# A convolution kernel's set-up: h's first FFT stage reads h in place, and table indices are made in another order

## The chip, the cores and the metric

One Trainium2 chip, one core of it. The metric is the device time of one execution in microseconds (us); the time before is the median of three runs. Five engines work side by side, each through its own queue in order: TensorE (PE; its weight loads are listed as PEld), VectorE (DVE), ScalarE (ACT), GpSimd (POOL) and SyncE (SP). TensorE writes its results to PSUM, from where VectorE or ScalarE move ("evict") them to SBUF.

## The reference, cut to what matters

```
# first part: a long causal convolution along the sequence, by FFT
B, S, D = 8, 5696, 128 ;  L = 2 * S
y = irfft(rfft(x, n=L, axis=1) * rfft(h, n=L, axis=0)[None], n=L, axis=1)[:, :S, :]
# second part, with x = y
theta  = x @ w_theta
zr, zi = x * cos(theta), x * sin(theta)
y = einsum('ts,bsd->btd', w_tok_r, zr) + einsum('ts,bsd->btd', w_tok_i, zi)
u = x + y
out = u + maximum(u @ w_ch, 0)
```

x is 8 x 5696 x 128 and h is 5696 x 128 in float32; w_tok_r and w_tok_i are 5696 x 5696. The change lies in the first part, and there in what is done once: the spectrum of h and the tables.

## The kernel before

**The FFT.** The length of 11392 is split into N1 = 178 and N2 = 64. The 5696 samples lie as NB = 89 partitions of N2 = 64 samples each. Stage a (`stage_a`) is a DFT over the 89 partitions: for each channel one product whose stationary operand (the weights) is the 89 x 128 block of data, and whose moving operand is the table f1_t (89 x 180, cosines and sines of K1 = 90 frequencies). Four channels make a chunk in one PSUM buffer of two banks; there are 16 chunks (64 channels) and four such buffers. Each chunk is evicted, with a change of layout, by ScalarE or by VectorE: `on_dve` lists the chunks that VectorE takes. Stage 2 (`f2`) multiplies by the table w_t2, 32 small products a chunk in 12 chunks (`CHK`), two halves of the array at a time. Stage b (`stage_b`) multiplies x's spectrum by h's into u_t and v_t (line 400, one product for each). Stages c and d go back to time.

**How h is treated.** h is loaded by two DMAs into the first 8192 columns of u_t (lines 122 to 125), as [n, half, d] in float16: 64 samples n, two halves of the channels, 64 channels d. VectorE then copies it (line 291) into h16 with the halves outermost, so that for each d the 128 weights (half, n) stand at one constant step. `h_chunk` evicts h's stage 2: ScalarE writes the real part to the tiles hs (line 326), VectorE the other part to h16 under the name h_later (line 327), which is used a second time for that. `h_other` exchanges halves by 18 DMAs on SyncE's queue, and `h_store` puts the rest in memory.

**The tables.** w_t2 is made in three parts: `w_turns`, `w_angles` and `w_sines`, and then on VectorE alone `w_rest` (lines 203 to 211), four instructions a part. `e_index` (three GpSimd instructions: iota, product, sum) makes the arguments for one of seven steps of the table e_t, and `e_table` turns them into sines on VectorE and ScalarE; four steps' arguments fit at a time, so steps 4 to 6 wait for earlier ones to be used. `r_table` makes the two small tables r_u and r_v; its arguments are seven GpSimd instructions each.

**What sets the order.** From line 143 on, VectorE, ScalarE and GpSimd run in the order of the program (a manual schedule). At line 486 GpSimd leaves that order and is placed by the scheduler; VectorE and ScalarE stay in it through stage b of the first group of x. There are eight groups of x (four pairs of batches, two halves of the channels); group 0's stage a is the list a0, its stage b is b0, and `load_x(1)` loads the next group into the same single buffer x16, 16 DMAs on GpSimd's queue. `woven` interleaves lists of steps by position.

Before the change the order is: the copy into h16; w_rest 1; h's stage a (chunks 4, 6, 8, 10, 12 and 14 on VectorE); w_rest 2; h's stage 2; e_index 0 to 3 and the arguments of r_table (which the scheduler puts among them on GpSimd, from 23.6 to 43.2 us); x's stage a with e_table 0 after its tenth chunk; load_x(1); e_index 4; stage b with r_table.

Of the kernel before, what the change touches and what calls it, by code (L numbers as in the profile page):

```python
# [10 lines left out]
F32 = mybir.dt.float32  # L11
# [12 lines left out]
def kernel(  # L24
# [10 lines left out]
    nc = tc.nc  # L35
    B, S, D = x.shape
    assert D == 128
    P = 128
# [119 lines left out]
    def up(t, k, eng=nc.vector):  # L158
        eng.tensor_scalar(k, t, MAGIC, None, op0=add)
# [43 lines left out]
    def w_rest(b):  # L203
        s0 = WS * b
        here = w_t2[:, s0:s0 + WS]
        two = here[:, :, :2 * N2].rearrange("p k (f a n) -> p k f a n", f=2, a=2)
        nc.vector.tensor_scalar(two[:, :, :, 1], two[:, :, :, 0], odd, None, op0=mult)
        nc.vector.tensor_scalar(here[:, :, 2 * N2:], here[:, :, :N2], -1.0, None, op0=mult)
        for p0 in (0, 64):
            nc.vector.tensor_copy(w_t2[p0:p0 + 64, KH + s0:KH + s0 + WS],  # L210
                                  w_t2[64 - p0:P - p0, s0:s0 + WS])
# [29 lines left out]
    def stage_a(lhs, on_dve=()):  # L241

        st = {}

        def chunk(q):
            if q == 0:
                st["a"] = fa.tile([P, 2 * K1, HD], F16, tag="a", name="a_")
            ps = psum()
            for i in range(4):
                nc.tensor.matmul(ps[:, i // 2, (i % 2) * 2 * K1:(i % 2 + 1) * 2 * K1], lhs(q + i), f1_t[:NB],  # L250
                                 start=True, stop=True)
            a_out = st["a"][:, :, q:q + 4].rearrange("p k (a q) -> p k a q", a=2)
            a_in = ps[:, :, :4 * K1].rearrange("p a (q k) -> p k a q", q=2)
            if q // 4 in on_dve:
                nc.vector.tensor_copy(a_out, a_in)
            else:
                nc.scalar.activation(a_out, a_in, AF.Copy)
        return [lambda q=q: chunk(q) for q in range(0, HD, 4)], st
# [28 lines left out]
    w_in = [s1.tile([P, P], F32, name=f"w_in{q}") for q in range(2)]  # L287
    for w_, t in ((moe_w_theta, w_in[0]), (moe_w_ch, w_in[1])):
        nc.gpsimd.dma_start(t, w_[:, :])
    for d0 in range(0, HD, 32):  # L290
        nc.vector.tensor_copy(h16[:NB, :, :, d0:d0 + 32],
                              u_t[:NB, :N2 * D].rearrange("p (n h d) -> p h n d", h=2, d=HD)[:, :, :, d0:d0 + 32])
    steps, a_h = stage_a(lambda q: h16[:NB].rearrange("p h n d -> p (h n) d")[:, :, q], (4, 6, 8, 10, 12, 14))
    w_rest(1)
    for f in steps:
        f()
    w_rest(2)

    nc.gpsimd.memset(u_t[:, UVW:], 0.0)
    nc.gpsimd.memset(v_t[:, UVW:], 0.0)  # L300
# [40 lines left out]
    e_t = fc.tile([P, EN, 2, NB], F16)  # L341
    sgn = fc.tile([P, N2], F32)

    def r_table(n_, r_):
        t, k = (s1.tile([P, 2 * N2], F32, name=f"r_{n_}{q}") for q in "tk")
        index(k, [[0, 2], [1, N2]], 0)
        nc.gpsimd.tensor_scalar(t, k, lane[:, 0:1], 1.0 / N2, op0=mult, op1=mult)
        for q0 in range(2):
            for q1 in range(2):
                a_ = t[64 * q0:64 * q0 + 64, 64 * q1:64 * q1 + 64]  # L350
                nc.gpsimd.tensor_scalar(a_, a_, 0.25 * (1 + (1 - n_ if q0 else n_) + q0 - q1), None, op0=add)
        up(t, k, nc.gpsimd)
        below_one(t, k)
        sine(k, t, 1)
        nc.scalar.activation(r_[:, :N2 + EN], k[:, :N2 + EN], AF.Copy, scale=0.125)
        nc.scalar.activation(r_[:, N2 + EN:], k[:, N2 + EN:], AF.Copy, scale=-0.125)
# [116 lines left out]
                h_other(c0, n)  # L473
    for c0, n in BATCH:
        h_store(c0, n)
    for e_ in E_STEPS[:4]:
        e_index(*e_)
    for t, dst, mul in ((w_in[0], w_theta_sb, 1.0 / (2.0 * math.pi)), (w_in[1], w_ch_sb, 1.0)):
        nc.gpsimd.tensor_scalar(dst, t, mul, None, op0=mult)
    for n, f in enumerate(a0):  # L480
# [1 line left out]
        if n == 9:  # L482
            e_table(*E_STEPS[0])
    load_x(1)
    e_index(*E_STEPS[4])
    in_order.close()
    in_order.enter_context(tc.manual_schedule(engines={mybir.EngineType.DVE, mybir.EngineType.Activation}))
    woven(b0, ([s_table, lambda: r_table(0, r_u), lambda: r_table(1, r_v)], 0.0, 0.6),
# [797 lines left out]
```

## Time and profile before

| | |
|---|---|
| median of 3 runs | 2045.61 us (2044.21 to 2046.22) |
| the profiled execution | 2043.46 us, span 2041.7 us, mean granted clock 0.986 |
| TensorE, VectorE, ScalarE, GpSimd busy | 95%, 77%, 32%, 48% of the span |
| h's load lands | 10.2 and 10.4 us after the issues at 1.28 and 2.32 us |
| h's stage a on TensorE | 16.09 to 25.9 us |
| h's stage 2 on TensorE | 26.79 to 35.9 us |
| x's stage a, stage b, stage c begin | 36.26, 45.13, 66.47 us |

Times in the profile are counted from the start of the span. "Idle before, with a releaser" names what ended a wait; a wait for several things is put down to the one that came last. Products are pipelined: the duration shown of one contains the way through the array, and the distance between starts says how fast they go. A granted clock of 0.50 is half clock. No clock event is recorded ahead of 32 us; the column reads 1.00 there whatever the clock was. In tile names the profile cuts digits: f_t is f1_t, h is h16, w_t is w_t2.

### The profile page before, as it was taken

To read this page: it belongs to the slowest core of one execution; us is meant where nothing else is said; L and a number is where in the kernel's file an instruction comes from. 1 tells how busy PE (TensorE), PEld (TensorE's weight loads), DVE (VectorE), ACT (ScalarE), POOL (GpSimd) and SP (SyncE) were. 2 spreads that over 40 slices of the span, in tenths; PEclk is the share of its full clock that TensorE was granted. 3 is DMA by queue.
4 is the path that set the end of the run, shared out by engine and by line. 5 is a ranking of instruction groups with operands and counts; after the bars stand their busy time and mean duration, and the time that the engine had idled before them with its cause. 6 is when DMAs were issued, how large, how long until landed. Compare 5 with 4: busy or idle time off the path is not lost.

```text
span 2041.7 us, 41287 instructions
## 1 busy us (share of the span) xinstructions
PE 1938.2 (95%) x15664; PEld 1074.5 (53%) x15841; DVE 1573.3 (77%) x2890; ACT 654.2 (32%) x1004; POOL 973.8 (48%) x1744
## 2 busy tenths in 40 slices
PE   5799999799999999999999998999999999999998
PEld 5688888654444444444444443444444444444444
DVE  8777778777788888888876757867777786777767
ACT  6788888862232333233200000011111111111111
POOL 8523421485353545454666454453544545354450
PEclk9799999899999999999999999999999999999999
DMA  9969975999898989999999799796977969788793
GB/s 117 62 74 130 92 83 167 262 264 187 158 178 174 175 170 168 176 174 180 166 168 157 121 258 210 111 154 125 154 139 133 160 123 155 132 148 145 133 156 85
DMA packets 491239, 312.56 MB, mean 153 GB/s; under 512 B 182983, under 2 KB 456007, under 8 KB 490055
## 3 DMA queue, kind: packets, MB, share of 16 engines
q0 software_dynamic: 322608, 158.13, 61.2%
q1 hardware_dynamic: 162448, 140.25, 24.2%
q10 hardware_dynamic: 5984, 11.54, 1.6%
q8 instruction: 124, 2.03, 0.4%
q14 instruction: 75, 0.61, 0.1%
HBM read 354.89 MB, written 90.82 MB: 218 GB/s over the span
## 4 chain that ended last, share of the span: by engine, by line
PE 63%; DVE 4%; DMA 3%; issue 2%; POOL 2%; ACT 0%; DVEq 0%; SPq 0%
PE m L1223 59%; POOL ring L627 2%; DVE c L1230 1%; DMA ring<-in_moe_w_tok_i_dram 1%; PE v L925 1%; PE utp L918 1%; PE m L1227 1%; DVE wt L838 1%; DVE b L776 1%; DMA ring<-in_moe_w_tok_r_dram 1%; PE theta_ps L514 0%; PE tpz L866 0%; DMA wl<-in_moe_w_tok_i_dram 0%; PE m L1110 0%; PE m L1144 0%
## 5 line engine op out<-in xcount | busy, mean ns | idle before, releaser
L627 POOL DMA_DIRECT2D ring<-in_moe_w_tok_i_dram x720 | 387.6, 546 | 652.4 <-DVE wt L838 581.6
L627 POOL DMA_DIRECT2D ring<-in_moe_w_tok_r_dram x720 | 386.6, 548 | 137.2 <-DVE wt L838 82.8
L838 DVE STREAM_TRANSPOSE wt<-ring 128x384 f32<-128x384 f32 (+2 forms) x720 | 359.5, 524 | 116.1 <-PE m L1223 67.5
L1223 PE MATMUL m<-b,wt 128*128 128x512 bf16 x1599 | 385.0, 379 | 4.2 <-DVE wt L838 1.7
L1223 PEld LDWEIGHTS <-wt 128*128 128x128 bf16 x1804 | 175.9, 98 | 218.8 <-DVE wt L838 7.5
L1230 DVE TENSOR_TENSOR c<-c,m 128x512 f32<-128x512 f32 x412 | 265.9, 671 | 0.4 <-PE m L1223 0.4
L920 ACT ACTIVATE ring<-utp 128x512 bf16<-128x512 bf16 x85 | 50.7, 597 | 582.2 <-PE utp L918 582.2
L137 POOL DMA_DIRECT2D x<-in_x_dram x128 | 99.1, 788 | 142.3 <-PE ps L250 132.4
L420 PE MATMUL ps<-r_u,u_t 128*128 128x128 f16 x1024 | 125.6, 221 | 5.3 <-DVE u_t L400 2.4
L421 PE MATMUL ps<-r_v,v_t 128*128 128x128 f16 x1024 | 124.6, 221 | 0.2
L915 ACT ACTIVATE ub<-c 128x512 bf16<-128x512 f32 x88 | 55.1, 628 | 192.1 <-DVE c L1185 113.5
L1144 PE MATMUL m<-b,wt 128*128 128x512 bf16 x465 | 109.8, 381 | 7.2 <-DMA b<-zz 2.7
L421 PEld LDWEIGHTS <-v_t 128*128 128x128 f16 x1024 | 101.1, 99 | 5.2 <-issue 3.7
L420 PEld LDWEIGHTS <-u_t 128*128 128x128 f16 x1024 | 101.2, 99 | 3.3 <-DVE u_t L400 3.3
L398 ACT ACTIVATE xs<-ps 128x1024 f16<-128x1024 f32 x96 | 91.6, 982 | 9.6 <-PE ps L274 3.3
L400 DVE TENSOR_TENSOR u_t<-xs,hs 128x1024 f16<-128x1024 f16 x96 | 64.3, 670 | 31.4 <-ACT xs L398 29.1
L1144 PEld LDWEIGHTS <-wt 128*128 128x128 bf16 x528 | 50.6, 98 | 67.4 <-issue 6.5
L516 ACT ACTIVATE red<-theta_ps,magic 128x512 f32<-128x512 f32 (+1 forms) x46 | 31.6, 687 | 137.0 <-PE theta_ps L514 102.8
L268 PEld LDWEIGHTS <-w_t 64*128 64x128 f16 x3240 | 58.9, 101 | 22.2 <-issue 16.4
L868 ACT ACTIVATE ring<-tpz 128x512 bf16<-128x512 bf16 (+1 forms) x46 | 27.5, 597 | 130.6 <-PE tpz L866 115.6
L400 DVE TENSOR_TENSOR v_t<-xs,hs 128x1024 f16<-128x1024 f16 x96 | 63.8, 665 | 0.0
L776 DVE TENSOR_TENSOR b<-b 128x1024 bf16<-128x1024 bf16 x100 | 61.4, 682 | 0.0
(2934 smaller groups left out, 3796.5 us busy)
## 6 DMA issues: line engine op xcount, KB each, us to landing
ring<-in_moe_w_tok_r_dram POOLq DMA_DIRECT2D x352, 96.0 KB, 4.5
ring<-in_moe_w_tok_i_dram POOLq DMA_DIRECT2D x352, 96.0 KB, 4.7
ring<-in_moe_w_tok_r_dram POOLq DMA_DIRECT2D x352, 80.0 KB, 4.4
ring<-in_moe_w_tok_i_dram POOLq DMA_DIRECT2D x352, 80.0 KB, 3.8
cp_hbm<-c SPq DMA_DIRECT2D x88, 256.0 KB, 2.5
c<-cp_hbm SPq DMA_DIRECT2D x88, 256.0 KB, 4.5
out_dram<-c SPq DMA_DIRECT2D x88, 256.0 KB, 4.2
yy<-y_hbm SPq DMA_DIRECT2D x84, 128.0 KB, 2.4
```

The source lines that it names most:

```text
L137: nc.gpsimd.dma_start(x16[p0:p1, e, n0:n0 + 16, :HD], bass.AP(tensor=src.tensor, offset=src.offset + (p0 * N2 + n0) * D + dh * HD, ap=[[N2 ...
L268: nc.tensor.matmul(ps[:, e, j * HD:(j + 1) * HD], w_t2[rows, slot(e, c0 + j), N2 * (1 - ri):N2 * (3 - ri)], a_st["a"][rows, ri * K1 + c0 + ...
L398: nc.scalar.activation(xs[:, :, :, :ck], ps, AF.Copy)
L400: nc.vector.tensor_tensor(uv[r][:, :, :, c0:c0 + ck], xs[:, :, :, :ck], hv[:, r:r + 1].to_broadcast([P, 2, HD, ck]), op=mult)
L420: nc.tensor.matmul(o, u_t[:, at:at + P], r_u, start=True, stop=False)
L421: nc.tensor.matmul(o, v_t[:, at:at + P], r_v, start=False, stop=True)
L627: nc.gpsimd.dma_start(wb[32 * i:32 * i + 32, :ng, :nj * 64], bass.AP(tensor=a.tensor, offset=a.offset + row0 * S + p * H + i * QR + j0 * 6 ...
L776: return [lambda f=f, x=x: f(*x) for f, x in ((nc.vector.tensor_sub, (bt[M3], b12, b22)), (nc.vector.tensor_sub, (bt[M4], b21, b11)), (nc. ...
L838: nc.vector.transpose(wt.rearrange("p j t r -> p (j t r)").bitcast(F32).rearrange("p (j g t) -> p g j t", j=TJ, g=4)[:, :ng, :nj], wb[:, : ...
L1144: nc.tensor.matmul(ms[n // 2 * 2 + h], a[n][:, j, :, r], bts_of[p][jj][n % 2 * 2 + h][:, r, :], start=(n % 2 == 0 and jj == 0 and r == 0), ...
L1223: nc.tensor.matmul(ms[q], a[q][:, j, :, r], bts[jj][q][:, r, :], start=(jj == 0 and r == 0), stop=(jj == NJ - 1 and r == 1 and q not in left))
L1230: nc.vector.tensor_tensor(c, z, ms[q], op=op)
```

## The change

Three things are changed. h's copy into h16 is left out: stage a takes a list of weights per channel, for h two 89 x 64 blocks straight from u_t (64 samples at a step of 128 elements), and multiplies each with f1_t into its own half of the output partitions; for x nothing changes. VectorE now takes chunks 11, 13 and 15 of h's stage a and ScalarE the other 13, and w_rest 1 and 2 are written after the fourth and the eighth chunk; on VectorE's queue that is w_rest 0, 1, 2 and then the three chunks. And on GpSimd's queue the arguments come as e_index 0, both r_table's (split off as `r_index`), e_index 1, the two weights, load_x(1), then e_index 2, 3 and 4.

```diff
@@ stage_a, chunk
-                nc.tensor.matmul(ps[:, i // 2, (i % 2) * 2 * K1:(i % 2 + 1) * 2 * K1], lhs(q + i), f1_t[:NB],
-                                 start=True, stop=True)
+                w_ = lhs(q + i)
+                if not isinstance(w_, list):
+                    w_ = [w_]
+                m = P // len(w_)
+                for e, w in enumerate(w_):
+                    nc.tensor.matmul(ps[m * e:m * e + m, i // 2, (i % 2) * 2 * K1:(i % 2 + 1) * 2 * K1], w, f1_t[:NB],
+                                     start=True, stop=True)
@@ h's first stage
-    for d0 in range(0, HD, 32):
-        nc.vector.tensor_copy(h16[:NB, :, :, d0:d0 + 32],
-                              u_t[:NB, :N2 * D].rearrange("p (n h d) -> p h n d", h=2, d=HD)[:, :, :, d0:d0 + 32])
-    steps, a_h = stage_a(lambda q: h16[:NB].rearrange("p h n d -> p (h n) d")[:, :, q], (4, 6, 8, 10, 12, 14))
-    w_rest(1)
-    for f in steps:
+    h_in = u_t[:NB, :N2 * D].rearrange("p (n h d) -> p h n d", h=2, d=HD)
+    steps, a_h = stage_a(lambda q: [h_in[:, e, :, q] for e in range(2)], (11, 13, 15))
+    for n, f in enumerate(steps):
         f()
-    w_rest(2)
+        if n in (3, 7):
+            w_rest(1 + n // 7)
@@ r_table
-    def r_table(n_, r_):
-        t, k = (s1.tile([P, 2 * N2], F32, name=f"r_{n_}{q}") for q in "tk")
+    r_in = {}
+
+    def r_index(n_):
+        t, k = r_in[n_] = [s1.tile([P, 2 * N2], F32, name=f"r_{n_}{q}") for q in "tk"]
         index(k, [[0, 2], [1, N2]], 0)
...
         up(t, k, nc.gpsimd)
+
+    def r_table(n_, r_):
+        t, k = r_in[n_]
         below_one(t, k)
@@ order
-    for e_ in E_STEPS[:4]:
-        e_index(*e_)
+    e_index(*E_STEPS[0])
+    r_index(0)
+    r_index(1)
+    e_index(*E_STEPS[1])
...
     load_x(1)
-    e_index(*E_STEPS[4])
+    for e_ in E_STEPS[2:5]:
+        e_index(*e_)
```

## The prediction

> **What bounds the kernel now.** I read the page first (shares, chain), then a table of stretches for the first 93 us, then the timelines of TensorE, VectorE, ScalarE and GpSimd over the same stretch, because the diff touches only the set-up.
>
> ```profile
> PE 1938.2 (95%) x15664; PEld 1074.5 (53%) x15841; DVE 1573.3 (77%) x2890; ACT 654.2 (32%) x1004; POOL 973.8 (48%) x1744
> ...
> PE 63%; DVE 4%; DMA 3%; issue 2%; POOL 2%; ACT 0%; DVEq 0%; SPq 0%
> ```
>
> TensorE is busy 95% of the span and carries the chain, so an edit of the set-up is worth what it lets TensorE's long stream start earlier, and no more. The set-up, by stretches (length, then PE, PEld, DVE, ACT, POOL busy, granted clock):
>
> ```profile
> 12.70:16.10 3.40, 0.01 (x1) 0.02 (x1) 3.36 (x4) 0.02 (x1) 2.85 (x4) 1.00 3.65 132
> 16.10:26.80 10.70, 9.84 (x66) 9.61 (x67) 10.02 (x13) 7.38 (x10) 10.43 (x16) 1.00 1.46 86
> 66.50:73.00 6.50, 6.49 (x55) 6.31 (x56) 3.84 (x6) 3.50 (x6) 2.54 (x3) 0.50 0.00 0
> 73.00:92.70 19.70, 16.63 (x296) 16.08 (x294) 17.49 (x22) 16.41 (x27) 11.66 (x16) 1.00 0.71 46
> ```
>
> TensorE does nothing until 16.1. The timelines (start, length, what, idle time before and its releaser) of TensorE, VectorE, ScalarE, GpSimd:
>
> ```profile
> 16.09 9.85 PE L250 MATMUL ps<-f_t,h 89*128 89x180 f16 x64 [16.09 <-DVE h L291]
> 26.79 6.79 PE L268 MATMUL ps<-a__184,w_t 64*128 64x64 f16 x287 [0.86 <-ACT a__184 L257]
> 36.26 5.92 PE L250 MATMUL ps<-f_t,x 89*128 89x180 f16 x56 [0.36 <-DVE h L327]
> 66.47 0.29 PE L420 MATMUL ps<-r_u,u_t 128*128 128x128 f16 x1 [0.87 <-DVE u_t L400]
> ```
> ```profile
> 14.49 2.71 DVE L291 COPY h<-u_t 89x4096 f16<-89x4096 f16 x2
> 26.20 0.48 DVE L207 TENSOR_SCALAR w_t<-w_t,lane 128x960 f16<-128x960 f16 x1
> 27.42 2.16 DVE L210 COPY w_t<-w_t 64x2880 f16<-64x2880 f16 x2
> 29.61 5.14 DVE L327 TENSOR_SCALAR h<-ps 128x512 f16<-128x512 f32 x8
> 35.52 2.08 DVE L327 TENSOR_SCALAR h<-ps 128x512 f16<-128x512 f32 x4 [0.77 <-ACT hs L326]
> 61.69 1.00 DVE L400 TENSOR_TENSOR u_t<-xs,hs 128x1024 f16<-128x1024 f16 x1
> ```
> ```profile
> 16.97 2.76 ACT L257 ACTIVATE a__184<-ps 128x720 f16<-128x720 f32 x4 [4.25 <-PE ps L250]
> ```
> ```profile
> 11.76 1.93 POOL L137 DMA_DIRECT2D x<-in_x_dram  x2 [1.74 <-DMA u_t<-in_h_dram]
> 60.46 1.70 POOL L371 TENSOR_SCALAR e_all<-e_all,lane 90x445 f32<-90x445 f32 x1
> ```
> ```profile
> 1172.18 0.59 PE L1110 MATMUL m<-b,wt 128*64 128x512 bf16 x2
> 1172.40 0.59 PE L1110 MATMUL m<-b,out__17518 128*64 128x512 bf16 x2
> ```
>
> To see there: h's first stage waits for the copy L291, though h itself is there earlier; its 64 products go at (9.85 - 0.36) / 63 = 0.150 us each, where x's of the same shape later take 0.077 (fifteen from 37.53 in 1.32, less the last one's 0.24). So TensorE runs at half clock from 16 to 26 (the column's 1.00 there only says that no clock event is recorded before 32). Half-clock products, not evictions, set that stage. Then VectorE owes the third part of w_t (26.20 to 29.58) before it can scale any of h's second stage, and it stays late until 37.6 (35.52 + 2.08).
>
> **The change, part by part.**
>
> *The copy L291 goes.* TensorE waits for h's load and for f1_t (ready at 9.8). The load's two pieces are issued at 1.28 and 2.32 and take 10.2 and 10.4 us, so the later lands at 12.7; GpSimd, which waits for both, goes on 0.28 after each landing. I put TensorE's start at 12.95 instead of 16.09: -3.14.
>
> *64 products become 128 of half width.* Two products with 64 columns each go to the two halves of the array. Nearest row: L1110, 64-column weights into the two halves; its groups of two start every 0.216 us (1172.18, 1172.40), which is what one 512-wide product of L1223 takes (18 in 3.88), so a pair costs one. Ends: 0.150 us a channel (pairs at once) and 0.300 (in turn). I take 0.150, by L1110, the one row with this layout; stage cost 0, the other end is a rival.
>
> *Evictions: 13 on ScalarE, 3 on VectorE (was 10 and 6); w_rest 1 and 2 ahead of VectorE's three.* ScalarE takes 0.69 a chunk (2.76 / 4), TensorE 0.60. A chunk can be evicted 0.88 after its start (16.97 - 16.09). ScalarE's first 11 chunks end at 13.83 + 11 x 0.69 = 21.4, hardly behind TensorE. VectorE ends w_rest 0 at 14.46 and needs 3.4 for each of the others (17.12 to 20.55 and 26.20 to 29.58 today): free at 21.3. Chunk 11 then holds its PSUM buffer until 22.2, chunk 15 needs that buffer (there are four), starts at 22.3 and is evicted 23.2 to 24.1. The second stage starts at 24.15, not 26.79: -2.64; half a microsecond of the first gain is lost to the late VectorE. If w_rest takes 3.0, as the first does, it is 0.3 better.
>
> *w_rest 2 no longer stands between.* At half clock a chunk of the second stage comes every 0.85 (ScalarE's evictions at 27.87, 28.72, 29.57). VectorE's first scaling starts 1.08 + 0.65 after the stage does, at 25.9, and takes 0.64 (5.14 / 8). Full clock came 5.2 after the stage's start (from 32.2 ScalarE's evictions come every 0.52, three in 1.57); I take 4.5, so five chunks at 0.85, then 0.64: 25.9 + 4 x 0.85 + 0.64 + 6 x 0.64 + 0.35 = 34.1 instead of 37.6: -3.5. Ends: full clock at once, 32.9 (-4.7); none, 35.6 (-2.0).
>
> *Behind it* nothing is new: x's first stage is bound by VectorE (seven casts and e_table), its x landed by 25.1, and GpSimd's indices are due later than they are ready. GpSimd's moved set: memsets end at 23.7, then e_index 0, both r_index, e_index 1, 2.7 + 3.3 + 3.3 + 2.7 + 1.1 for the two weights = 37; load_x(1), which today starts at 44.57 behind TensorE's last reading of x16, could start at 41.1 and is not held up. SyncE's 18 exchanges of h (31.05 to 45.04) start with ScalarE's fourth chunk at 28.4 and stay ahead of their readers (the fifth chunk's at 51.8). So the -3.5 holds at stage b's start.
>
> *e_index 2 and 3 fall behind load_x(1)*, into the products u_t and v_t of L400, beside e_index 4, which is there today. Today GpSimd's two passes ran 1.70 and 1.66 instead of 0.64 and 1.33, and two of L400's products 1.00 and 1.04 instead of 0.69: 0.65 lost for one e_index. load_x(1) now ends at 56.3 and VectorE's last product at 63: two of the three fit in, one more than today, +0.65. Ends: 0 (the load ends late) and +3.4 (every product under them at 1.0). r_table's order on VectorE and ScalarE is unchanged.
>
> *Stage C's half clock.* It starts at 66.47 and runs at 0.50 to 73.0. [...]
>
> **Sum.** -3.5 + 0.65 - 0.25 = -3.1. The profiled execution took 2043.46 (span 2041.7 and 1.76 around it); it would be 2040.4. The median of the runs stands 2.15 above it, 2045.61; so 2042.5. All that follows stage C hangs on TensorE's order and moves with it. 0.2% is 4.1 us, about what a measurement can tell from no change: my sum is just inside.
>
> **Rivals.**
>
> *The halves go in turn (slower).* For it: L1110 shows only 512-wide products; here a product is 180 wide, and a 64-column weight load took 106 to 110 ns there, no less than the 98 of a 128-column one, so two unhidden loads are 0.22 a channel, over the 0.150. Against: the loads of L1110 start in pairs too. Fully in turn: 128 x 0.150 = 19.2, second stage at 33.4 instead of 24.15, -3.1 + 9.25 = +6.1: 2051.7. It turns the sign from 0.20 us a channel (64 x 0.05 = 3.1) and passes 4.1 from 0.26.
> [...]
>
> *Full clock comes with the first stage (faster).* What raises the clock is not seen. L250's stream left it at half for 9.6 us; L268's, two products in flight at a time, raised it in 5.2. If products in flight count, the paired first stage raises it; if rows in use count (89 of 128, against 128), it does not. Evictions would hold the first stage at 24.1 all the same; the second would end at 32.9: 1.2 more, -4.3: 2041.3, and sooner still if stage C gains too.
> [...]
>
> *GpSimd gives it back (no change).* All three e_index beside L400 at the dear end: -3.5 + 3.4 - 0.25 = -0.35: 2045.3. For it: 1.00 against 0.69; against: only two of some six products under e_index 4 were slow.
>
> **Chances.** My sum 0.64, of which 0.27 beyond 4.1 us (the clock's ends), 0.36 within, 0.01 slower; full clock early 0.14, faster; given back 0.06, same; halves in turn 0.16, slower. Faster 0.41, same 0.42, slower 0.17. The sum's own ends add up to 2038.8 and 2047.5. The range 2039.0 to 2047.5 leaves out nearly all of the slower rival and a few in a hundred at the low end.
>
> **What would show it.** First L250 product at about 12.95 released by h's load; its pairs every 0.150; second stage at 24.1; last L327 by 34.1; load_x(1) at 41; L400 slow at more than two products; stage C at 63.6. Wrong if L250's stage lasts over 13 us, if half clock in stage C lasts longer than today, or if a wait takes over between 34 and 63.

## The result and the profile after

The changed kernel takes 2046.62 us (median; 2041.22 to 2049.29) against 2043.61 us of the kernel before on the same chip (2039.71 to 2046.28). The ratio is 1.0013, with a 95% interval of 1.0007 to 1.0019: some 2.7 us slower (the medians alone differ by 3.0), less than the 0.2% that the prediction took as its bound. The profiled execution after took 2045.08 us, with a span of 2043.3 us; that of before 2043.46 and 2041.7.

First the page after: the line of busy times, and the chain of work that ended last.

```profile
PE 1950.7 (95%) x15905; PEld 1076.4 (53%) x15905; DVE 1571.4 (77%) x2885; ACT 656.2 (32%) x1007; POOL 971.3 (48%) x1744
...
PE 67%; DVE 3%; DMA 2%; issue 1%; POOL 0%; ACT 0%; DVEq 0%; SPq 0%; ACTq 0%
```

TensorE still carries the chain, with 12.5 us more of busy time (1950.7 against 1938.2). The set-up has 64 more weight loads and 64 more products (before's trace lacks some 180 records of products: it has 15841 loads for 15664 of them). VectorE is busy 1.9 us less.

TensorE's timeline after, over the set-up (start, length, what, in brackets the idle time before and what ended it):

```profile
12.69 8.67 PE L255 MATMUL ps<-f_t,u_t 89*64 89x180 f16 x112 [12.69 <-DMA u_t<-in_h_dram]
22.69 1.47 PE L255 MATMUL ps<-f_t,u_t 89*64 89x180 f16 x16 [1.33 <-DVE a__178 L260]
25.16 7.89 PE L273 MATMUL ps<-a__178,w_t 64*128 64x64 f16 x351 [1.00 <-DVE a__178 L260]
35.21 0.32 PE L273 MATMUL ps<-a__178,w_t 64*128 64x64 f16 x9 [2.15 <-issue]
35.69 0.82 PE L255 MATMUL ps<-f_t,x 89*128 89x180 f16 x8 [0.16 <-issue]
36.82 8.36 PE L255 MATMUL ps<-f_t,x 89*128 89x180 f16 x56 [0.32 <-DVE h L330]
```

VectorE's, ScalarE's and GpSimd's, a few lines of each:

```profile
15.84 2.26 DVE L210 COPY w_t<-w_t 64x2880 f16<-64x2880 f16 x2
19.44 2.26 DVE L210 COPY w_t<-w_t 64x2880 f16<-64x2880 f16 x2
21.73 1.72 DVE L260 CAST a__178<-ps 128x720 f16<-128x720 f32 x2
36.08 0.89 DVE L330 TENSOR_SCALAR h<-ps 128x512 f16<-128x512 f32 x2 [1.91 <-ACT hs L329]
63.66 1.07 DVE L408 TENSOR_TENSOR u_t<-xs,hs 128x1024 f16<-128x1024 f16 x1
```
```profile
13.60 8.06 ACT L262 ACTIVATE a__178<-ps 128x720 f16<-128x720 f32 x12 [0.88 <-PE ps L255]
```
```profile
45.48 6.18 POOL L137 DMA_DIRECT2D x<-in_x_dram  x8 [9.59 <-PE ps L255]
59.62 0.62 POOL L155 IOTA e_all<- 90x445 f32 x1
```

To see there: the first product comes at 12.69, released by h's load, and its pairs go at once. A wait for VectorE follows, of 1.33, where the prediction had about half a microsecond, and stage 2 begins at 25.16. Then, nine products before the end of stage 2, TensorE stands still for 2.15 us with nothing that the profile shows to wait for ("issue"), and VectorE's last two scalings wait with it. Finally x's first stage, of the same products as before, takes from 35.69 to 46.04, where it took from 36.26 to 45.13. The same stretches side by side (length; busy time of PE, PEld, DVE, ACT, POOL with instructions; granted clock; DMA share; GB/s), before and after:

```profile
31.00:36.00 5.00, 3.82 (x215) 3.73 (x210) 4.12 (x7) 3.31 (x8) 4.71 (x7) 1.00 0.67 150
36.00:45.00 9.00, 6.41 (x64) 5.57 (x64) 8.36 (x13) 8.17 (x13) 6.92 (x13) 1.00 0.39 83
```
```profile
31.00:36.00 5.00, 2.67 (x133) 2.30 (x125) 3.08 (x5) 2.67 (x7) 4.46 (x7) 1.00 0.69 154
36.00:45.00 9.00, 8.68 (x63) 8.40 (x61) 7.45 (x11) 7.24 (x12) 0.00 (x0) 0.56 0.46 111
```

In x's first stage TensorE had full clock before (1.00) and mostly half clock after (0.56): 64 products fill 6.41 us there and 63 fill 8.68 here. The half clock comes 13.7 us long, from 37.1. VectorE, which bound that stage before, is now less busy than TensorE.

How the lead is lost, from the first products to the second group of x (us; both kernels were profiled twice; the second profiles' figures stand after the stroke):

| | before | after | later by |
|---|---|---|---|
| h's first stage starts | 16.09 / 16.04 | 12.69 / 12.74 | -3.40 / -3.30 |
| h's stage 2 starts | 26.79 / 26.75 | 25.16 / 25.17 | -1.63 / -1.58 |
| last scaling of h ends | 37.60 / 37.85 | 36.97 / 37.85 | -0.63 / 0.00 |
| stage b starts on TensorE | 45.13 / 45.39 | 46.04 / 47.22 | +0.91 / +1.83 |
| first product u_t | 46.87 / 47.12 | 48.17 / 49.35 | +1.30 / +2.23 |
| last product v_t ends | 66.72 / 66.98 | 69.49 / 69.85 | +2.77 / +2.87 |
| second group's first u_t | 93.78 / 92.94 | 96.23 / 96.38 | +2.45 / +3.44 |

The set-up is thus +2.9 us later by the mean of the two, about what the whole kernel is.

**Where TensorE's instructions come from.** The trace's DMA records hold transfers of 16384 bytes on the queue named "q8 instruction"; the page counts them in its list of queues, before and after:

```profile
q8 instruction: 124, 2.03, 0.4%
```
```profile
q8 instruction: 125, 2.05, 0.4%
```

TensorE's products and loads number some 31,700 and 31,810, which over 124 and 125 transfers is about 255 a transfer; the 128 products between two stops of one stage (after product 223 and 351 in the second profile of after, below) make it 256. That this queue carries TensorE's instructions is taken from the count and from the times below. The records around the two stops, and what TensorE did (start and length of the transfer in us; entry is when TensorE begins the last block that it still has):

```
         entry   transfer        ends    runs dry   goes on
before   31.15   32.08 + 1.06    33.14   33.58      34.66
after    30.67   32.25 + 1.34    33.59   33.06      35.21
```

So in both the transfer began while TensorE used the block before (0.93 and 1.58 us after the entry), and TensorE went on 1.5 to 1.6 us after the transfer's end, 3.5 (before) or 4.5 us (after) after the entry. But the block of these small products, 128 of them with their loads, was used up in 2.4 us. That is the stop, and before's profile has it too, 1.08 us long, after product 287:

```profile
34.66 1.24 PE L268 MATMUL ps<-a__184,w_t 64*128 64x64 f16 x73 [1.08 <-issue]
```

The change adds 128 instructions ahead (64 loads and 64 products), so the blocks end 64 products earlier: after 223 and, one block on, after 351 of the 360.

From this came the theory that the experiments test. (1) The place of the stop follows the count of TensorE's instructions, and the stop replaces what was to be won. (2) The half clock in x's first stage goes with it. (3) The order of the indices costs products of u_t and v_t. Against it stood: that the reading in place, or VectorE's new order, is itself the loss; and that the half clock is mere timing.

### The profile page after: what moved, and what is told of

It is laid out like the page before. It is cut to its first block, busy times and chain, and to the rows that moved or that the text cites. A ratio compares the mean times of both kernels' runs of the same rounds, so it can differ in the third digit from the quotient of the medians.

```text
span 2043.3 us, 41593 instructions
## 1 busy us (share of the span) xinstructions
PE 1950.7 (95%) x15905; PEld 1076.4 (53%) x15905; DVE 1571.4 (77%) x2885; ACT 656.2 (32%) x1007; POOL 971.3 (48%) x1744
## 4 chain that ended last, share of the span: by engine, by line
PE 67%; DVE 3%; DMA 2%; issue 1%; POOL 0%; ACT 0%; DVEq 0%; SPq 0%; ACTq 0%
PE m L1234 62%; DVE b L787 1%; DVE c L1241 1%; PE v L936 1%; PE utp L929 1%; PE m L1238 1%; DMA b<-z_hbm 1%; DMA ring<-in_moe_w_tok_i_dram 1%; DVE wt L849 1%; POOL ring L638 0%; PE theta_ps L525 0%; PE tpz L877 0%; PE m L1121 0%; PE m L1155 0%; DMA wl<-in_moe_w_tok_i_dram 0%
## 5 line engine op out<-in xcount | busy, mean ns | idle before, releaser
L1234 PE MATMUL m<-b,wt 128*128 128x512 bf16 x1640 | 390.1, 380 | 2.0 <-DVE wt L849 1.7
L1155 PE MATMUL m<-b,wt 128*128 128x512 bf16 x480 | 112.0, 383 | 6.2 <-DVE wt L849 4.2
```

What stands on the lines that cost most here:

```text
L1155: nc.tensor.matmul(ms[n // 2 * 2 + h], a[n][:, j, :, r], bts_of[p][jj][n % 2 * 2 + h][:, r, :], start=(n % 2 == 0 and jj == 0 and r == 0), ...
L1234: nc.tensor.matmul(ms[q], a[q][:, j, :, r], bts[jj][q][:, r, :], start=(jj == 0 and r == 0), stop=(jj == NJ - 1 and r == 1 and q not in left))
```

## The experiments

The markers of all of them, in us from the span's start; "stop" is TensorE's idle time at a block's end in h's stage 2, with the product that it follows; "half" is where the half clock after it begins, and how long it lasts; "slow" counts the products of u_t and v_t in the first group that took about 1.0 instead of 0.69:

| kernel | stage 2 starts | stop | scalings end | half | stage b | u_t, v_t last (slow) | second group |
|---|---|---|---|---|---|---|---|
| before | 26.79 | 1.08 @287 | 37.60 | 45.7, 3.4 | 45.13 | 19.85 (2) | 93.78 |
| before, again | 26.75 | 1.17 @287 | 37.85 | 46.1, 3.4 | 45.39 | 19.85 (2) | 92.94 |
| after | 25.16 | 2.15 @351 | 36.97 | 37.1, 13.7 | 46.04 | 21.32 (6) | 96.23 |
| after, again | 25.17 | 2.87 @351 | 37.85 | 36.5, 13.7 | 47.22 | 20.50 (4) | 96.38 |
| index order put back | 24.97 | 2.59 @351 | 36.95 | 34.6, 17.1 | 46.28 | 19.18 (0) | 94.28 |
| index order alone | 26.83 | 1.66 @287 | 37.60 | 37.0, 13.7 | 46.87 | 20.90 (4) | 96.63 |
| after + 128 instructions | 25.07 | 1.77 @287 | 36.04 | 35.2, 13.7 | 45.32 | 20.90 (4) | 94.99 |
| before + 128 instructions | 27.10 | 2.31 @351 | 38.97 | 37.5, 13.7 | 48.37 | 19.19 (0) | 96.43 |
| reading in place alone | 24.71 | 3.11 @351 | 37.55 | 36.9, 13.7 | 46.83 | 19.18 (0) | 95.23 |
| VectorE's order alone | 27.12 | 1.01 @287 | 37.30 | 44.5, 3.4 | 44.84 | 19.84 (2) | 93.55 |
| after, old index order, + 128 | 25.19 | 0.65 @287 | 34.97 | 42.2, 3.4 | 42.50 | 19.84 (2) | 91.21 |
| the same, again | 25.18 | none | 35.21 | 41.3, 6.8 | 43.03 | 19.85 (2) | 91.25 |
| the same, wide products | 25.17 | none | 35.27 | 41.3, 6.8 | 43.09 | 19.84 (2) | 91.27 |
| the same, + 64 | 24.87 | 1.90 @319 | 36.01 | 35.6, 13.7 | 45.29 | 19.48 (1) | 93.96 |

The added instructions are products of one column, each with its weight load, into a PSUM buffer that nobody reads, ahead of h's first stage. A ratio with its interval is not the quotient of the two medians beside it and can differ from that by 0.001.

### The index order put back

```diff
     def r_table(n_, r_):
+        r_index(n_)
         t, k = r_in[n_]
...
-    e_index(*E_STEPS[0])
-    r_index(0)
-    r_index(1)
-    e_index(*E_STEPS[1])
+    for e_ in E_STEPS[:4]:
+        e_index(*e_)
...
-    for e_ in E_STEPS[2:5]:
-        e_index(*e_)
+    e_index(*E_STEPS[4])
```

> The changed kernel with GpSimd's old order of the arguments (e_index 0 to 3 and both r_index ahead, only e_index 4 behind load_x(1)). Theory: the three e_index beside L400's products cost stage b 1.5 us (six products of about 1.04 instead of two), so from the first to the last of L400's first group takes 19.8 us as before the change instead of 21.3, and the kernel comes out 1.5 us faster than the changed one: a ratio to the kernel before of about 1.0006. What lies ahead of stage b stays as in the changed kernel (the pause of TensorE of about 2.2 us before the last products of h's stage 2, half clock in x's first stage). Rival: stage b is longer for another reason (half clock in its products); then it stays at 21.3 and the ratio at 1.0013.

Measured: 2046.96 us against 2046.03, ratio 1.0003 (0.9992 to 1.0015). The products of u_t and v_t last 19.18 us, none slow; the second group comes at 94.28, 2.0 ahead of after. The median doesn't tell it from either kernel. The counts of one line, after and here:

```profile
L408 DVE TENSOR_TENSOR u_t<-xs,hs x12: 380/690/1076, 48.2 to 68.8; 128x1024 f16<-128x1024 f16 x11, 128x256 f16<-128x256 f16 x1
```
```profile
L409 DVE TENSOR_TENSOR u_t<-xs,hs x12: 383/691/696, 48.4 to 66.9; 128x1024 f16<-128x1024 f16 x11, 128x256 f16<-128x256 f16 x1
```

The longest of them is 1076 ns with the new order and 696 with the old one. Stop and half clock stay, so they aren't the index order's.

### The index order alone, in the kernel before

```diff
-    for e_ in E_STEPS[:4]:
-        e_index(*e_)
+    e_index(*E_STEPS[0])
+    r_index(0)
+    r_index(1)
+    e_index(*E_STEPS[1])
...
-    e_index(*E_STEPS[4])
+    for e_ in E_STEPS[2:5]:
+        e_index(*e_)
```

with `r_index` split off as in after, and nothing else.

> The kernel before with the new order of the arguments alone. Theory: stage b's products take 21.3 us instead of 19.8, all else as before, the ratio about 1.0007. Rival, that the order is harmless where nothing else is moved: 19.8 and 1.0000.

Measured: 2047.61 against 2046.03, ratio 1.0008 (0.9995 to 1.0021). The products last 20.90 with four slow ones, 1.05 more than before. But the stop was 1.66 here, at the same place as before, and x's first stage ran at half clock from 37.0:

```profile
34.66 1.24 PE L268 MATMUL ps<-a__184,w_t 64*128 64x64 f16 x73 [1.66 <-issue]
36.26 9.75 PE L250 MATMUL ps<-f_t,x 89*128 89x180 f16 x64 [0.36 <-DVE h L327]
```

Up to there TensorE's program is before's own. So the half clock is not tied to the reading in place; what differs is the length of the stop.

### The block's end moved back: after, with 128 more instructions

```diff
+    pre = psum()
+    for n in range(64):
+        nc.tensor.matmul(pre[:, 0, :1], ident_bf, ident_bf[:, :1], start=True, stop=True)
     steps, a_h = stage_a(lambda q: [h_in[:, e, :, q] for e in range(2)], (11, 13, 15))
```

> The changed kernel with 64 products of one column each (and their weight loads) on TensorE while it waits for h anyway: 128 more instructions ahead, nothing read from them. Theory: TensorE's pause of 2.15 us before the last 9 products of h's stage 2 is a wait for its instructions, which come in blocks of 256; 128 instructions more put the end of the block 128 earlier, so the pause comes after about 287 of the 360 products (where the kernel before has its pause of 1.08 us) and lasts 1.0 to 1.5 us, the window behind it is not empty, half clock does not return at 37, and the kernel is 1 to 2.5 us faster than the changed one (ratio 0.9998 to 1.0008). Rival: the pause belongs to its place in the program (evictions or SyncE's exchanges); then it stays before the last 9 products at about 2.2 us and the ratio at 1.0013.

Measured: 2044.51 against 2046.03, ratio 1.0001 (0.9987 to 1.0014). The stop is back at product 287:

```profile
25.07 6.25 PE L273 MATMUL ps<-a__243,w_t 64*128 64x64 f16 x287 [1.00 <-DVE a__243 L260]
33.09 1.25 PE L273 MATMUL ps<-a__243,w_t 64*128 64x64 f16 x73 [1.77 <-issue]
```

That is half of the theory. The stop was longer than expected, 1.77, and the half clock stayed (from 35.2): the expectation that it would go with the place was wrong. The second group came 1.24 earlier than in after.

### The block's end moved on: before, with 128 more instructions

```diff
+    pre = psum()
+    for n in range(64):
+        nc.tensor.matmul(pre[:, 0, :1], ident_bf, ident_bf[:, :1], start=True, stop=True)
     steps, a_h = stage_a(lambda q: h16[...][:, :, q], (4, 6, 8, 10, 12, 14))
```

> The mirror of the run with shifted boundary: the kernel before with the same 64 one-column products ahead of h's first stage, in time that TensorE waits anyway. Theory: the pause of 1.08 us after 287 products of h's stage 2 moves to before the last 9 or so, as the changed kernel has it, and lasts 0 to 2 us, since VectorE's backlog lets TensorE take that block more slowly; the time changes by less than 1.5 us. Rival: the pause stays after 287 products.

Measured: 2047.36 against 2046.03, ratio 1.0006 (0.9991 to 1.0021). The stop is longer than the 0 to 2 us expected.

```profile
27.10 7.81 PE L268 MATMUL ps<-a__249,w_t 64*128 64x64 f16 x351 [0.86 <-ACT a__249 L257]
37.23 0.30 PE L268 MATMUL ps<-a__249,w_t 64*128 64x64 f16 x9 [2.31 <-issue]
```

Products that compute nothing give the kernel before the stop of after, at the same product, and its half clock: scalings 1.4 later, stage b 3.2 later, the second group 2.7 later. (The products of u_t and v_t gave 0.66 of it back.) None of the change is in this kernel.

### The kernel before, unchanged, once more

> The kernel before, profiled once more, nothing changed. Question: whether half clock in x's first stage, which the profile of the changed kernel has from 37 on and the first profile of the kernel before only from 45.7 on, belongs to the change. Theory: it doesn't; it hangs on where the clock's windows of 3.4 us fall, and the kernel before has it too in some executions (the one with the new order of arguments alone had it from 37.0 on). Then here half clock from 35 to 38, stage b's first product near 48.5 to 49 and its second group's near 95.5. Rival: the kernel before keeps full clock until 45.7 and its second group starts at 93.8, as in its first profile.

Measured: 2048.87 us for this one run. The set-up is as in the first profile, with a stop of 1.17 and full clock in x's first stage:

```profile
34.92 1.24 PE L268 MATMUL ps<-a__184,w_t 64*128 64x64 f16 x73 [1.17 <-issue]
36.52 5.92 PE L250 MATMUL ps<-f_t,x 89*128 89x180 f16 x56 [0.36 <-DVE h L327]
```

The expectation of half clock here was wrong. Two profiles don't rule chance out, though: how a stop of this length lies to the clock's own steps may matter too (last section). What the profiles so far had in common was the stop's length: 1.08 and 1.17 with full clock, 1.66 and more with half.

### The reading in place alone

```diff
+    h_in = u_t[:NB, :N2 * D].rearrange("p (n h d) -> p h n d", h=2, d=HD)
-    steps, a_h = stage_a(lambda q: h16[:NB].rearrange("p h n d -> p (h n) d")[:, :, q], (4, 6, 8, 10, 12, 14))
+    steps, a_h = stage_a(lambda q: [h_in[:, e, :, q] for e in range(2)], (4, 6, 8, 10, 12, 14))
```

with the copy gone; w_rest, evictions and indices as before.

> The kernel before with h read in place in half-width products, nothing else: evictions (six on VectorE), the order of w_rest and the arguments as before. Theory: TensorE starts at 12.7, but VectorE is in w_rest 1 until 18.1, so chunk 4 holds its buffer until 19.1 and the second stage starts at about 25.2, no earlier than in the changed kernel; w_rest 2 then delays the scalings, which end near 37 (37.0 there, 37.6 before); the pause is before the last 9 products of h's stage 2, 2 to 2.8 us. Stage b loses nothing. In all 0 to 1 us slower than before (ratio 1.0000 to 1.0005). Rival, the sum of the prediction: 2.5 us faster, 0.9988.

Measured: 2044.21 against 2043.94, ratio 0.9995 (0.9984 to 1.0007).

```profile
24.71 7.97 PE L273 MATMUL ps<-a__182,w_t 64*128 64x64 f16 x351 [0.86 <-ACT a__182 L262]
35.80 0.32 PE L273 MATMUL ps<-a__182,w_t 64*128 64x64 f16 x9 [3.11 <-issue]
```

Stage 2 starts 2.08 earlier than in before, and the scalings end only 0.05 earlier: the stop, 3.11, takes all of it. Without VectorE's new order stage 2 even starts 0.45 earlier than in after.

### VectorE's order alone

```diff
-    steps, a_h = stage_a(lambda q: h16[...][:, :, q], (4, 6, 8, 10, 12, 14))
-    w_rest(1)
-    for f in steps:
+    steps, a_h = stage_a(lambda q: h16[...][:, :, q], (11, 13, 15))
+    for n, f in enumerate(steps):
         f()
-    w_rest(2)
+        if n in (3, 7):
+            w_rest(1 + n // 7)
```

> The kernel before with the new division of evictions (three on VectorE) and w_rest 1 and 2 ahead of them, h still copied, one product a channel, arguments in the old order. Theory: the second stage starts at about 27.1, 0.3 later than before; the scalings are no longer behind w_rest 2 and end near 36.5 instead of 37.6, less what the pause for instructions (after 287 products, as before, 1.3 to 2 us) takes; in all 0.5 to 1 us faster than before, ratio 0.9995 to 1.0000. Rival: VectorE's backlog was hidden by the pause anyway; no change.

Measured: 2044.26 against 2043.94, ratio 0.9995 (0.9983 to 1.0008). The scalings end at 37.30, 0.30 before those of before, not the 1.1 expected. w_rest 2 is out of the way, but the stop is not, and the scalings wait for the 73 products behind it:

```profile
34.36 1.24 PE L268 MATMUL ps<-a__180,w_t 64*128 64x64 f16 x73 [1.01 <-issue]
```

The count of TensorE's instructions, and with it the place of the stop, is before's; the full clock is too, and the stop's length all but so.

### What is left when the stop is short: after, with the old index order and 128 more instructions

```diff
+    pre = psum()
+    for n in range(64):
+        nc.tensor.matmul(pre[:, 0, :1], ident_bf, ident_bf[:, :1], start=True, stop=True)
...
-    e_index(*E_STEPS[0])
-    r_index(0)
-    r_index(1)
-    e_index(*E_STEPS[1])
+    for e_ in E_STEPS[:4]:
+        e_index(*e_)
...
-    for e_ in E_STEPS[2:5]:
-        e_index(*e_)
+    e_index(*E_STEPS[4])
```

with `r_table` as in the first experiment.

> The changed kernel with both of the losses found so far taken away: the old order of the arguments, and 64 one-column products ahead so that the end of a block of instructions falls after 287 of the 360 products of h's stage 2. Theory: second group of x about 93.3, that is 1.7 earlier than with the shifted boundary alone (95.0); the time 1 to 2.5 us below the kernel before, ratio 0.9988 to 0.9997. Rival: the two losses aren't independent (a later load of x meets the products anyway): 95.0 and a ratio of 1.0001.

Measured: 2042.15 against 2043.94, ratio 1.0001 (0.9990 to 1.0012).

```profile
25.19 6.17 PE L273 MATMUL ps<-a__243,w_t 64*128 64x64 f16 x287 [1.00 <-DVE a__243 L260]
32.02 1.25 PE L273 MATMUL ps<-a__243,w_t 64*128 64x64 f16 x73 [0.65 <-issue]
33.63 5.93 PE L255 MATMUL ps<-f_t,x 89*128 89x180 f16 x56 [0.36 <-DVE h L333]
```

With a stop of 0.65 the scalings end at 34.97, x's first stage has full clock, stage b starts at 42.50 and the second group at 91.21: 2.57 earlier than in before, where 93.3 had been expected. The convolution's last product v_t ends at 334.33 against 338.67 and 340.08 in before. In the median of the runs nothing of it can be told.

> The same kernel as in the run without the new order and with the shifted boundary, measured once more beside the kernel before, since its first interval did not settle it. Theory: 1 to 2.5 us faster than before, ratio 0.9988 to 0.9997, second group of x at 91 to 93.5. Rival: no difference, 1.0000.

The same kernel once more: 2042.48 against 2043.13, ratio 0.9998 (0.9985 to 1.0010). Stage 2 ran through (no stop), the second group came at 91.25, the last product v_t ended at 334.68:

```profile
25.18 8.38 PE L273 MATMUL ps<-a__243,w_t 64*128 64x64 f16 x360 [1.00 <-DVE a__243 L260]
```

So the lead in the set-up repeats, and again none can be told at the end.

### Wide products ahead, to raise the clock

```diff
     for n in range(64):
-        nc.tensor.matmul(pre[:, 0, :1], ident_bf, ident_bf[:, :1], start=True, stop=True)
+        if n < 40:
+            nc.tensor.matmul(pre[:, 0, :1], ident_bf, ident_bf[:, :1], start=True, stop=True)
+        else:
+            nc.tensor.matmul(pre[:, n % 2, :], ident_bf, ident_bf[:, :1].to_broadcast([P, 512]), start=True, stop=True)
```

> As the run without the new order and with the shifted boundary, but 24 of the 64 products ahead are 512 columns wide, so that TensorE is busy until h has landed and the clock is full when h's first stage starts. Theory: h's products come every 0.077 us a pair, evictions bound the stage and it ends no earlier (second stage at 24.3 to 25.2); the second stage then uses up a block of instructions faster than the next one comes (3.5 to 4.5 us after the block before was entered), so pauses grow by what the clock gives, and the scalings end at 34 to 35, no more than 1 us earlier; ratio within 0.0005 of the kernel without the wide products. Rival: the clock is what bounds the second stage; then it ends 2 us earlier, with scalings at 33, and the time falls by 2.

Measured: 2042.72 against 2043.13, ratio 0.9992 (0.9982 to 1.0002). The wide products keep TensorE busy from 3.51 to 10.65, and an idle 2.10 us follow, in which it waits for ScalarE and h's load; 1.3 us into h's first stage, at 14.0, the clock is at half, and it stays so to 31.1:

```profile
3.51 7.14 PE L301 MATMUL ps<-ident_bf 128*128 128x512 bf16 x24
12.75 8.39 PE L255 MATMUL ps<-f_t,u_t 89*64 89x180 f16 x112 [2.10 <-ACT w_t L171]
25.17 8.39 PE L273 MATMUL ps<-a__243,w_t 64*128 64x64 f16 x360 [1.00 <-DVE a__243 L260]
```
```profile
10.00:14.00 4.00, 1.90 (x26) 1.38 (x25) 3.47 (x6) 3.24 (x6) 1.83 (x3) 1.00 3.08 109
14.00:24.00 10.00, 8.44 (x111) 8.06 (x108) 9.20 (x11) 7.94 (x13) 10.00 (x15) 0.50 1.90 115
```

TensorE was busy 8.44 of the 10 us from 14 on, and had half clock in all of them. Whether the clock fell by the idle 2.10 or by the stage's own products isn't told apart; that the stage did not raise it is shown (0.50 from 14 to 24). What full clock in the two stages would be worth is therefore not tested. The short time ahead of 14.0, still at full clock, shows something else:

```profile
12.75 1.55 PE L255 MATMUL ps<-f_t,u_t 89*64 89x180 f16 x22 [2.10 <-ACT w_t L171]
```
```profile
L255 PEld LDWEIGHTS <-u_t x24: 185/207/210, 12.7 to 14.0; 89*64 89x64 f16 x24
```

These eleven pairs come every 0.11 us ((1.55 - 0.35) / 10.5, with 0.35 as the length of the last), each behind two weight loads of 0.207. Expected was 0.077, which a full-width product of x takes at full clock. At full clock a pair is dearer than one full-width product (0.11 against 0.077); at half clock it is not (0.151 in after against 0.150 in before). Scalings, stage b and second group are the narrow products' to 0.1 us. The clock event at 14.0 also says, for the first time in this case, that the clock is at half ahead of 31, where the prediction had inferred it from the products' spacing.

### 64 more instructions instead of 128

```diff
     pre = psum()
-    for n in range(64):
+    for n in range(32):
```

in the kernel with the old index order and the narrow products.

> The changed kernel in the old order of arguments with 32 one-column products ahead, 64 instructions. Theory: the pause comes after 319 of the 360 products of h's stage 2, half way between the two places seen so far (287 and 351), and lasts 0.8 to 2.5 us. Rival: it stays at 287 or 351.

Measured: 2048.78 us for the one run.

```profile
24.87 6.89 PE L273 MATMUL ps<-a__211,w_t 64*128 64x64 f16 x319 [1.00 <-DVE a__211 L260]
33.66 0.78 PE L273 MATMUL ps<-a__211,w_t 64*128 64x64 f16 x41 [1.90 <-issue]
```

Half the instructions move the stop by half the way, to product 319. The stop is 1.90, and with it come the half clock and a second group 2.7 later than with 128.

### The kernel after, unchanged, once more

> The changed kernel, profiled once more. [...] Rival: the half clock of its first profile was a matter of the windows' place, and it is full here until stage b, second group at 94.5.

Measured: 2045.69 us for the one run. The stop of 2.87 is at 351 again, with a small one ahead of it, at the block's end before:

```profile
25.17 5.46 PE L273 MATMUL ps<-a__178,w_t 64*128 64x64 f16 x223 [1.00 <-DVE a__178 L260]
30.99 2.23 PE L273 MATMUL ps<-a__178,w_t 64*128 64x64 f16 x128 [0.36 <-issue]
36.09 0.32 PE L273 MATMUL ps<-a__178,w_t 64*128 64x64 f16 x9 [2.87 <-issue]
```

The middle line is one block from end to end: 128 products with their loads in 2.23 us. The transfer that it waits for ran from 33.42 to 34.71, and TensorE went on 1.38 after it.

## Why the prediction was wrong, by its own steps

The prediction said 3.1 us faster, and it is some 2.7 slower. The first profiles of the two kernels give the account: stage b was to start 3.5 earlier, at 41.63, and starts at 46.04. Of the 4.41 between, 1.01 is the late start of stage 2, 1.86 is the end of the scalings behind it, 1.48 is x's first stage, and 0.06 what is left.

- **The copy L291 goes: right.** 12.69, where 12.95 was predicted, released by h's load.
- **128 products of half width: right.** 56 pairs in 8.67 us are (8.67 - 0.36) / 55 = 0.151 a pair, as 0.150 was predicted. The rival that the halves go in turn would have made 0.300, and falls. The weight loads are hidden: two of 0.214 us each (by the mean) leave the pair at 0.151, where one of 0.174 and one product made 0.150 before. That holds for half clock alone, and so "a pair costs one" was right by the clock that the stage had: in the kernel with the wide products the pairs at full clock came every 0.11, between the 0.077 of one product and twice that.
- **Evictions: sign right, size off.** ScalarE kept up (12 chunks in 8.06). VectorE's w_rest 1 and 2 took 3.6 each, not 3.4, so it was free at 21.73 instead of 21.3. And TensorE waited for VectorE's eviction of chunk 11 with chunk 14 already (22.69), not with chunk 15, so two chunks of 0.6 came behind that wait instead of one; it waited 1.33, and stage 2 came at 25.16, not 24.15. The gain is 1.63, not 2.64. The reading in place alone has it at 24.71: the new order on VectorE makes the start later, not earlier.
- **"w_rest 2 no longer stands between": this is the step that failed.** VectorE was to end the scalings at 34.1 and ends at 36.97 and 37.85, a gain of 0.63 and none. VectorE is not what they wait for; they wait for TensorE, and TensorE for its next block. Where the stop is short or absent (0.65, none), the scalings end at 34.97 and 35.21: the step's 34.1 and the 1.0 by which stage 2 started late, to 0.1. So its working holds without the stop. The fault was a reading of before: that VectorE "stays late until 37.6" behind w_rest 2. The prediction's own line at 35.52 says that VectorE had caught up and sat idle 0.77 until ScalarE had evicted the next products; and those came from TensorE's 73 products behind the stop, at 34.66. So in before already the last four scalings waited for TensorE, and w_rest 2 hid only a part of the stop. That is why VectorE's order alone, with w_rest 2 out of the way, won only 0.30. The stop was in the trace of before, and the prediction left it out. One of the prediction's own signs of being wrong, a wait that takes over between 34 and 63, is what came.
- **"Behind it nothing is new": failed too.** x's first stage was bound by VectorE at full clock, 8.87 us; at half clock TensorE binds it, 10.35 (and 10.66 in the second profile). In the kernels here a stop of 1.17 or less goes with full clock there, without exception, and one of 1.66 or more with half, also in kernels without the change (the index order alone; before with 128 instructions).
- **e_index 2 and 3 fall behind load_x(1): mechanism right, size inside its ends.** +0.65 was predicted; the products last 21.32 and 20.50 instead of 19.85, so +1.47 and +0.65. By kernel, six slow products make 21.32, four 20.50 to 20.90, two 19.85, none 19.18: about 0.35 each. In after they lie in pairs at 60.5, 63.7 and 66.9, each beside GpSimd's product and sum of one e_index; in its second profile the first e_index ran while VectorE was idle, and two fewer were slow. load_x(1) did not start at 41.1 but at 45.48, since TensorE read x16 until then.
- **Stage C's half clock: not tested.** It was to begin 2.9 earlier and began 2.8 later (69.26). From its start to the second group it took 27.31 and 26.21 before, 26.97 and 26.76 after: the two profiles of before lie further apart than the -0.25 taken. No run shows that -0.25; what the first profiles show is that half clock lasted 6.51 us from the stage's start before (66.47 to 72.98) and 5.35 after (69.26 to 74.61).
- **The rivals.** Full clock with the first stage falls: pairs at 0.151 are half clock, and in the kernel with the wide products the clock event says so. Some 10 us of stage a's 89-row products did not raise it (0.50 from 14 to 24 us there). That GpSimd gives the gain back was a part of what happened, 0.65 to 1.47 us of it. No rival was the wait that TensorE has for its own instructions. (The sum's dear end is too high: -2.0 and +3.4 give 2047.0, not 2047.5, and for stage C no run shows a term.)

The experiments show the stop, the half clock that goes with a long one, and the index order as the losses in the set-up. The end is another matter. The set-up's +2.9 at the second group is of the size of the +2.7 at the end, but that after's loss in the set-up is its loss at the end is argued, not shown: at the convolution's last product v_t the profiles have +1.7 (341.31 and 340.76 against 338.67 and 340.08). And where the set-up was 2.6 earlier, no gain at the end could be told from none. The three such measurements (1.0001, 0.9998, 0.9992) lie nearer to none than to 2.6 us, which would be 0.9987; the interval of the first leaves that out, those of the other two don't. Between the profiles the stretch from the first weight transpose of the second part to the sixty-first, some 180 us long, varies from 176.9 to 186.3, and that from 1205 to 1356 us by 4, whatever the kernel, while that from 570 to 1205 is 635.1 to 635.2 in all. Whether an early set-up is given back in those stretches, or is only drowned by them, stays open. So does why the time from the entry of a block to the use of the next is 3.5 us in the first profile of before and 4.5 in that of after: of the difference, 0.65 lies ahead of the transfer and 0.28 in it.

## What to carry to other kernels

Ask what stands behind a stall before booking its end as a gain: here the `issue` wait of 1.08 us in TensorE's timeline was real, and hidden in part by w_rest 2 until that cover was gone. An engine that is idle for a while ahead of its last work is no longer late by what it owed before. Count instructions, not only their time: here splitting the products added loads and products that cost nothing in their own stage (0.151 us a pair against 0.150, at half clock) and moved the ends of the 256-instruction blocks in another one (from product 287 to 351); a block of short ones (128 products with their loads in 2.23 us) was used up faster than the next one came (3.0 to 5.4 us after its entry). And an idle time on TensorE may be paid a second time, by the clock of the stage behind it: here stops of 1.66 us and more were followed by half clock in x's first stage, those of 1.17 and less by full clock.

## What the runs showed of the hardware

- TensorE's instructions came in transfers of 16384 bytes, 256 instructions by the count (31,700 over 124 transfers, 31,810 over 125; 128 products with their loads between two stops); around the stops of the two first profiles the transfer of the next block began 0.93 and 1.58 us after the entry of the one in use. Over the twelve profiles with a stop, 3.0 to 5.4 us passed from the entry of a block to the use of the next, and TensorE went on 1.3 to 1.7 after the transfer's end. The last block of small products ahead of the stop lasted 2.2 to 2.7, so TensorE stopped for 0.65 to 3.11, at places that moved with the count (in the changed kernel 287, 319 and 351 with 128, 64 and no added instructions). The length varied at one place too (none to 1.77 at 287, 2.15 to 3.11 at 351), but every stop at 351 was longer than every one at 287: there the transfer began 1.6 to 2.6 us after the entry, at 287 and 319 0.65 to 1.5. What holds it back is not shown.
- A one-column product with its load cost TensorE 29 ns a pair (after + 128 instructions):

```profile
2.43 1.86 PE L298 MATMUL ps<-ident_bf 128*128 128x1 bf16 x64 [2.43 <-POOL ident_bf masks.py:199]
```

  64 took 1.86 us, in a time when TensorE had nothing else to do.
- Half clock was not only a matter of idle time here: with the wide products ahead TensorE had it for 10 us (14 to 24) in which it was busy 84%, to 21.1 without a gap, with products that use 89 of 128 rows. That the rows in use decide it is argued, not shown: no run changed the rows alone.
- How a stop leads to half clock can be followed some way. Every clock record of the fourteen profiles but a profile's last lasts a whole multiple of 3.41 us (3.41, 13.65 and 20.48 among those of both first profiles), so the clock was seen to change at the ends of such stretches only. In the eight profiles with half clock in x's first stage TensorE was busy 13 to 54% of the stretch that ends where it begins; in the six others the stretches with the stop, or in its place, were busy 66% or more. The nearest two (PE's busy time stands behind the length) are the index order alone and before's second profile:

```profile
33.60:37.00 3.40, 1.85 (x79) 1.79 (x79) 2.00 (x4) 1.93 (x5) 3.13 (x5) 1.00 0.63 152
```
```profile
32.50:35.90 3.40, 2.23 (x152) 2.12 (x148) 2.25 (x5) 2.17 (x5) 3.23 (x6) 1.00 0.83 187
```

  So where the stretch falls may count beside the stop's length, though no run shifted it alone: from 33.5 to 36.9 TensorE was busy 1.83 of 3.40 us in before's first profile as well, but there that was no stretch of the clock. Nor is the busy share the whole rule, since 66% was followed by full clock here, and 67 and 69% in x's first stage by half clock at 41.3 in the two kernels without a stop.
